# Sparse attention and spectral mix on one core: the first value rows through SyncE as fp32, rounded on chip

## The chip, the cores and the metric

The kernel runs on one core of one Trainium2 chip. The metric is the device time of one execution in microseconds (us). The number quoted for the kernel before is the median of three runs: 428.08 us, from 427.69 to 428.46 us.

## The reference, cut to what matters

Two stages follow one another. The first is a sparse attention over 8 batches, 8 heads, 576 positions and 64 columns. Heads 0 to 3 see the last 32 positions ("local"), heads 4 to 7 see every 32nd position ("strided"). The second stage treats the result as x (8 x 576 x 512): it takes a real Fourier transform along the sequence, multiplies the lowest 64 modes by complex 512 x 512 matrices, transforms back, adds, and applies one more matrix.

```python
mask_local = (rel >= 0) & (rel < stride)
mask_strided = (rel >= 0) & (pos[None, :] % stride == pos[:, None] % stride)
scores = np.where(masks[None, :, :, :], scores, -1000000000.0)
attn = softmax(scores); attn_out = np.matmul(attn, v)
...
X = np.fft.rfft(x, axis=1)
Yr = np.einsum('bmd,mde->bme', Xr, w_r) - np.einsum('bmd,mde->bme', Xi, w_i)
Yi = np.einsum('bmd,mde->bme', Xr, w_i) + np.einsum('bmd,mde->bme', Xi, w_r)
y = np.fft.irfft(Y, n=S, axis=1)
u = x + y
return u + np.maximum(u @ w_ch, 0.0)
```

Inputs and outputs are fp32. The two weight tensors w_r and w_i hold 64 x 512 x 512 numbers each, 134 MB together, and make up most of what is read.

## The kernel before, in words

All matmuls run in fp16 with fp32 sums. Every large input is therefore rounded on its way into SBUF, by a transfer that GpSimd issues (`nc.gpsimd.dma_start` from an fp32 tensor into an fp16 tile). These transfers form one list in program order on one queue, called q0 in the profile: first the strided rows of q, k and v, then, interleaved by hand, the weights (`w_fetch`, lines 182 to 190), the local rows (`load_loc`, line 229) and more strided rows. Eight semaphores are used in rotation, so a transfer of this list is issued only when the one eight places before it has landed. Some transfers also wait until TensorE has finished with the buffer that they overwrite.

The strided rows of one batch and one of q, k, v make a tile of 72 partitions by 2048 columns in `ring`: a partition holds 32 consecutive positions of one head. `load_str(b, nb)` loads partitions 0 to 63 with one transfer (line 220 for one batch, line 218 for two at once) and, for even b, partitions 64 to 71 of both batches of the pair with another (line 222, here called the tail, 64 KB in fp16). For b = 0 the list begins: v rows 0 to 63 (256 KB in fp16), v tail, q rows, q tail, k rows, k tail; then v, q and k rows of batch 1 without tails; then the pair of batches 2 and 3.

The constants lie in DRAM as fp16 and go through the two other queues: cI (identity for the transposes), cM6 and cM5 (masks of the strided scores) by ScalarE (q10 in the profile), cT (the Fourier table) and cMl (mask of the local scores) by SyncE (q1). After the rows of batch 1 GpSimd itself runs `strided_tokens` (lines 327 to 329), two memsets and a copy of cT, which has to have landed; the transfers that come later in its list stand behind that copy.

The computation of batch 0 begins with transposes of v (`str_v`, lines 276 to 283, in three column groups `JG` of 6, 5 and 5 blocks of 128 columns), which need rows and tail of v and cI. Ahead of them in program order VectorE clears `kzs[0]` (line 794). Later the strided stage runs over the 8 batches, then the local stage together with the first weights (`mode`, matmuls of line 597), then the second half of the weights, and at the end the last modes (line 630), the inverse transform and the output.

The weight tiles have five buffers of their own and three guests: the tile of mode pair 7 lies under the tag "YT" of the pool `big`, which later holds a spectrum.

Of the kernel before, what the change touches and what calls it, by code (L numbers as in the profile page):

```python
# [10 lines left out]
FP = mybir.dt.float32  # L11
# [12 lines left out]
JG = [(0, 6), (6, 11), (11, 16)]  # L24
# [32 lines left out]
def kernel(  # L57
# [10 lines left out]
    nc = tc.nc  # L68
# [3 lines left out]
    big = ctx.enter_context(tc.tile_pool(name="big", bufs=1))  # L72
# [5 lines left out]
    def psum_pools(**bufs):  # L78
        pctx.close()
        pss.clear()  # L80
        for n, c in bufs.items():
            pss[n] = pctx.enter_context(
                tc.tile_pool(name="ps_" + n, bufs=c, space=PSUM)
            )
# [22 lines left out]
    def const_load(eng, *which):  # L107
        for n in which:
            eng.dma_start(cs[n][:, 0 : hosts[names.index(n)].shape[1]], drams[n])
# [93 lines left out]
    def str_in(b, vi):  # L203
        return ring[0:72, 3 * (b % 4) + SLOT[vi], :]

    def loc_in(b, vi):
        t = ring[:, ds(2 * (b % 6), 2), :].rearrange("p n x -> p (n x)")
        return t[:, ds(1152 * vi, 1152)]

    def load_str(b, nb):  # L210
        for vi in (2, 0, 1):
            n = 3 * (b % 4) + SLOT[vi]
            two = ring[:, n : n + 4 : 3, :]
            src = SRC[vi][b - b % 2 : b - b % 2 + 2, 4:8].rearrange(
                "b h (c r) d -> (h c) b (r d)", r=32
            )
            if nb == 2:
                nc.gpsimd.dma_start(two[0:64], src[0:64])
            else:
                nc.gpsimd.dma_start(ring[0:64, n, :], src[0:64, b % 2])  # L220
            if b % 2 == 0:
                nc.gpsimd.dma_start(two[64:72], src[64:72])
# [27 lines left out]
    def act_copy(out, in_):  # L250
        nc.scalar.activation(out=out, in_=in_, func=ACTF.Copy)  # L251
# [511 lines left out]


    psum_pools(tp=3, sc=3, av=2)
    load_str(0, 1)
    const_load(nc.scalar, "cI", "cM6", "cM5")
    load_str(1, 1)
    const_load(nc.sync, "cT", "cMl")
    strided_tokens()  # L770
    load_str(2, 2)
    w_fetch()

    def str_front(b):
        return [
            lambda: str_v(b, 0), lambda: str_v(b, 1),
            lambda: str_v(b, 2), lambda: str_q(b, 0),
            lambda: str_back(b, 0),
            lambda: str_back(b, 1), lambda: str_q(b, 1),
            lambda: str_k(b, 0),  # L780
            lambda: str_k(b, 1), lambda: str_k(b, 2),
        ]

    def loc_front(b):
# [6 lines left out]
            lambda: loc_back(b, 0), lambda: loc_back(b, 1),  # L791
        ]

    nc.vector.memset(kzs[0], 0.0)
    first = str_front(0)
    for i, w in enumerate(first):
# [170 lines left out]
    for n, i in enumerate([3, 5, 7] + list(range(8, 21))):  # L967
        b, t = n // 2, n % 2 * 2
# [144 lines left out]
```

## Time and profile before

| what | value |
|---|---|
| median of 3 runs | 428.08 us (427.69 to 428.46) |
| span of the profiled execution, first to last instruction | 426.7 us |
| median less span | 1.4 us |
| PE busy | 346.4 us (81%) |
| DVE / ACT / POOL busy | 234.7 / 218.3 / 110.7 us |
| time that packets of q0 took, as a share of 16 DMA engines | 96.2% |
| read from HBM | 162.83 MB |

The profile gives the span of one execution; no separate total for that execution is given, so the 1.4 us between its span and the median of the runs is taken as what lies around it. PE is TensorE, DVE VectorE, ACT ScalarE, POOL GpSimd and SP SyncE. "Idle before, releaser" tells which instruction or transfer ended an engine's idle time. The bytes of the DMA rows are those written: a rounding transfer reads twice as many as it writes.

### The profile page before, as it was taken

To read this page: it belongs to the slowest core of one execution; us is meant where nothing else is said; L and a number is where in the kernel's file an instruction comes from. 1 tells how busy PE (TensorE), PEld (TensorE's weight loads), DVE (VectorE), ACT (ScalarE), POOL (GpSimd) and SP (SyncE) were. 2 spreads that over 40 slices of the span, in tenths; PEclk is the share of its full clock that TensorE was granted. 3 is DMA by queue.
4 is the path that set the end of the run, shared out by engine and by line. 5 is a ranking of instruction groups with operands and counts; after the bars stand their busy time and mean duration, and the time that the engine had idled before them with its cause. 6 is when DMAs were issued, how large, how long until landed. Compare 5 with 4: busy or idle time off the path is not lost.

```text
span 426.7 us, 9768 instructions
## 1 busy us (share of the span) xinstructions
PE 346.4 (81%) x4167; PEld 208.2 (49%) x4167; DVE 234.7 (55%) x466; ACT 218.3 (51%) x390; POOL 110.7 (26%) x196
## 2 busy tenths in 40 slices
PE   2977878769999698889768788878788867889993
PEld 2866767554656365566433344435444423445330
DVE  3788778851355154356113246746676354655884
ACT  1687678643656356556642235423442444443872
POOL 8332333322423222222222322222232222210000
PEclk9999899967999689999995889989999979989997
DMA  8999999999999999999999999999999999995698
GB/s 150 210 212 212 213 213 213 211 211 211 214 213 213 213 213 215 212 214 215 210 214 211 213 214 213 210 213 215 212 213 214 213 213 214 214 212 105 244 355 287
DMA packets 30938, 91.62 MB, mean 215 GB/s; under 512 B 4464, under 2 KB 5232, under 8 KB 30896
## 3 DMA queue, kind: packets, MB, share of 16 engines
q0 software_dynamic: 25168, 81.28, 96.2%
q1 hardware_dynamic: 4976, 9.13, 5.9%
q10 hardware_dynamic: 752, 0.61, 0.5%
q8 instruction: 32, 0.52, 0.5%
q14 instruction: 10, 0.08, 0.0%
HBM read 162.83 MB, written 9.44 MB: 404 GB/s over the span
## 4 chain that ended last, share of the span: by engine, by line
DMA 47%; PE 29%; DVE 14%; ACT 5%; issue 3%; DVEq 0%; POOL 0%; ACTq 0%; POOLq 0%
DMA wt<-in_moe_w_i_dram 38%; DMA wt<-in_moe_w_r_dram 7%; PE y L597 5%; DVE xb L241 3%; DVE kz L283 3%; PE p L987 2%; ACT X L251 2%; PE sc L532 2%; PE tp L413 2%; PE sc L459 1%; PE p L1001 1%; PE y L532 1%; PE p L760 1%; DVE yy L752 1%; DVE rec L240 1%
## 5 line engine op out<-in xcount | busy, mean ns | idle before, releaser
L597 PE MATMUL y<-wt,X 128*32 128x512 f16 (+1 forms) x448 | 70.9, 430 | 20.1 <-DMA wt<-in_moe_w_i_dram 20.1
L186 POOL DMA_DIRECT2D wt<-in_moe_w_r_dram x59 | 34.7, 588 | 126.4 <-PE y L597 56.3
L186 POOL DMA_DIRECT2D wt<-in_moe_w_i_dram x60 | 35.4, 590 | 68.3 <-DMA wt<-in_moe_w_i_dram 44.4
L597 PEld LDWEIGHTS <-X 128*32 128x32 f16 (+1 forms) x448 | 28.1, 140 | 39.4 <-DMA wt<-in_moe_w_i_dram 18.6
L727 DVE COPY xo<-tp 128x512 f16<-128x512 f16 x32 | 22.1, 691 | 36.8 <-PE tp L725 36.8
L726 ACT ACTIVATE v<-sc 128x512 f16<-128x512 f32 x32 | 19.1, 597 | 44.2 <-PE sc L717 44.2
L717 PE MATMUL sc<-w_cp,xT 128*128 128x512 f16 x128 | 36.9, 410 | 1.9 <-DVE xT L690 1.9
L489 ACT ACTIVATE PL<-sc 128x480 f16<-128x480 f32 (+1 forms) x48 | 27.0, 578 | 21.3 <-PE sc L475 21.0
L241 DVE TENSOR_TENSOR xb<-av,rec 90x256 f16<-90x256 f32 (+2 forms) x80 | 36.0, 450 | 2.8
L240 DVE RECIPROCAL rec<-av 90x4 f32<-90x4 f32 (+2 forms) x80 | 14.6, 183 | 39.3 <-PE av L504 28.2
L251 ACT ACTIVATE yr<-y 128x512 f16<-128x512 f32 x28 | 16.7, 597 | 36.8 <-PE y L597 35.6
L961 DVE TENSOR_TENSOR xo<-p,xo 128x1024 f16<-128x1024 f32 x16 | 19.6, 1225 | 21.7 <-PE p L760 21.7
L420 DVE COPY qT<-tp 128x576 f16<-128x576 f16 x16 | 11.9, 752 | 34.7 <-PE tp L413 34.7
L251 ACT ACTIVATE v<-p 128x1024 f16<-128x1024 f32 x16 | 16.4, 1023 | 23.1 <-PE p L760 23.1
L378 ACT ACTIVATE PL<-sc 90x360 f16<-90x360 f32 (+1 forms) x48 | 22.7, 490 | 7.0 <-PE sc L371 6.4
L251 ACT ACTIVATE v<-tp 128x640 f16<-128x640 f16 (+1 forms) x24 | 19.0, 807 | 11.8 <-PE tp L447 9.3
L413 PE MATMUL tp<-cI_s,ring 64*64 64x64 f16 x864 | 22.4, 197 | 2.7 <-DVE qT L420 2.4
L459 PE MATMUL sc<-cMl_s,cI_s 128*128 128x480 f16 (+1 forms) x48 | 19.4, 405 | 4.5 <-ACT PL L489 2.9
L276 PE MATMUL tp<-cI_s,ring 72*128 72x72 f16 x256 | 15.4, 207 | 8.7 <-DMA ring<-in_v_dram 7.1
L413 PEld LDWEIGHTS <-ring 64*64 64x64 f16 x864 | 17.5, 110 | 9.4 <-issue 5.4
L251 ACT ACTIVATE kz<-tp 64x360 f16<-64x360 f16 (+1 forms) x32 | 18.9, 592 | 6.2 <-PE tp L413 5.2
L1013 ACT ACTIVATE rl<-p 128x1024 f32<-128x1024 f32 (+1 forms) x19 | 18.4, 979 | 5.7 <-PE p L1001 3.1
(142 smaller groups left out, 737.9 us busy)
## 6 DMA issues: line engine op xcount, KB each, us to landing
wt<-in_moe_w_i_dram POOLq DMA_DIRECT2D x60, 512.0 KB, 18.8
wt<-in_moe_w_r_dram POOLq DMA_DIRECT2D x59, 512.0 KB, 17.7
out_dram<-osb SPq DMA_DIRECT2D x15, 512.0 KB, 3.4
ring<-in_v_dram POOLq DMA_DIRECT2D x8, 288.0 KB, 13.4
ring<-in_q_dram POOLq DMA_DIRECT2D x8, 288.0 KB, 13.6
ring<-in_k_dram POOLq DMA_DIRECT2D x8, 288.0 KB, 13.1
ring<-in_v_dram POOLq DMA_DIRECT2D x3, 512.0 KB, 14.8
ring<-in_q_dram POOLq DMA_DIRECT2D x3, 512.0 KB, 14.8
```

The source lines that it names most:

```text
L186: nc.gpsimd.dma_start(dst, rows)
L241: nc.vector.tensor_tensor(out=dst, in0=val.rearrange("p h (q c) -> p h c q", c=4), in1=rec[0:n, 0:pieces] .to_broadcast((n, pieces, 64)) . ...
L251: nc.scalar.activation(out=out, in_=in_, func=ACTF.Copy)
L378: nc.scalar.activation(out=PS[0:n, ds(POFF[t], 4 * n)], in_=scp[0:n, 0 : 4 * n], func=ACTF.Exp, scale=SCALE,)
L413: nc.tensor.transpose(tp[ds(64 * hp, 64), ds(64 * i, 64)], qn[ds(64 * hp, 64), ds(64 * (9 * g + i), 64)], idn[ds(64 * hp, 64), ds(64 * hp, ...
L459: nc.tensor.matmul(scp[:, 0 : n * times].rearrange("p (h x) -> p h x", h=times), idn, mask_rows("cMl", n, times), start=True, stop=False,)
L489: nc.scalar.activation(out=dst, in_=src, func=ACTF.Exp, scale=SCALE)
L597: nc.tensor.matmul(yp[ds(a, 32), :], Xh[half][pr, c].rearrange("p b r (h m) -> p (b r h) m", h=2)[:, :, mm % 32], wt[pr, XC[c], :], start= ...
L717: nc.tensor.matmul(vp, xT[:, ch], w_chs["cp"][:, ch, :], start=(ch == 0), stop=(ch == 3),)
L726: nc.scalar.activation(out=v0, in_=vp, func=ACTF.Copy)
L727: nc.vector.tensor_copy(out=xo.rearrange("p (h q c) -> p h q c", h=2, c=4), in_=tp[:, 0:512].rearrange("p (h c q) -> p h q c", h=2, c=4),)
L961: nc.vector.tensor_tensor(out=xo, in0=up[:, 0:n], in1=xo, op=AluOp.add)
```

## The change

The v rows 0 to 63 of batch 0 leave GpSimd's list. SyncE loads them as fp32, without rounding, into a new tile `first32` (128 x 2048 fp32, of which 64 partitions are used) as the first transfer of its queue, ahead of cT and cMl. Three copies then round them into their place in `ring`, one for each column group: groups 0 and 2 on VectorE, group 1 on ScalarE. The copies stand ahead of the clearing of `kzs[0]` in program order. GpSimd's list now begins with the v tail, followed by the q rows. `first32` uses the tag "YT", so that the weight tile of mode pair 7 comes after it in the same memory.

```diff
+    first32 = big.tile([128, 2048], FP, tag="YT", name="first32")
+
+    def first_rows():
+        src = v[0, 4:8].rearrange("h (c r) d -> (h c) (r d)", r=32)
+        nc.sync.dma_start(first32[0:64], src[0:64])
+
+    def first_round(j):
+        cols = ds(128 * JG[j][0], 128 * (JG[j][1] - JG[j][0]))
+        dst, src = str_in(0, 2)[0:64, cols], first32[0:64, cols]
+        if j == 1:
+            act_copy(dst, src)
+        else:
+            nc.vector.tensor_copy(out=dst, in_=src)
+
     def load_str(b, nb):
...
             if nb == 2:
                 nc.gpsimd.dma_start(two[0:64], src[0:64])
-            else:
+            elif b or vi != 2:
                 nc.gpsimd.dma_start(ring[0:64, n, :], src[0:64, b % 2])
...
     psum_pools(tp=3, sc=3, av=2)
+    first_rows()
     load_str(0, 1)
     const_load(nc.scalar, "cI", "cM6", "cM5")
...
+    for j in range(3):
+        first_round(j)
     nc.vector.memset(kzs[0], 0.0)
```

## The prediction

> **What bounds the kernel now.** I read the page first: its DMA rows and its chain.
>
> ```profile
> DMA  8999999999999999999999999999999999995698
> q0 software_dynamic: 25168, 81.28, 96.2%
> DMA 47%; PE 29%; DVE 14%; ACT 5%; issue 3%; DVEq 0%; POOL 0%; ACTq 0%; POOLq 0%
> ```
>
> The DMA engines are busy from the second slice to the 36th, nearly all of it in GpSimd's queue q0, and DMA is the largest share of the chain. A busy share can still hide holes, so next comes the table by stretches (columns: stretch and its length, then PE, PEld, DVE, ACT and POOL busy time with counts, the granted clock, the DMA share, GB/s written).
>
> ```profile
> 1.50:2.00 0.50, 0.00 (x0) 0.00 (x0) 0.50 (x1) 0.00 (x0) 0.50 (x2) 1.00 0.46 58
> 2.00:2.50 0.50, 0.00 (x0) 0.00 (x0) 0.14 (x1) 0.39 (x1) 0.50 (x2) 1.00 0.83 255
> 2.50:3.00 0.50, 0.00 (x0) 0.00 (x0) 0.00 (x0) 0.50 (x1) 0.50 (x2) 1.00 1.54 267
> 3.00:3.50 0.50, 0.00 (x0) 0.00 (x0) 0.00 (x0) 0.40 (x1) 0.50 (x2) 1.00 1.07 66
> 3.50:4.00 0.50, 0.00 (x0) 0.00 (x0) 0.00 (x0) 0.00 (x0) 0.50 (x2) 1.00 0.24 33
> 4.00:4.50 0.50, 0.00 (x0) 0.00 (x0) 0.00 (x0) 0.00 (x0) 0.50 (x2) 1.00 0.95 164
> ...
> 110.00:160.00 50.00, 44.80 (x698) 28.36 (x696) 21.86 (x44) 28.23 (x55) 14.49 (x25) 0.90 1.07 213
> 210.00:260.00 50.00, 38.51 (x293) 19.45 (x294) 16.92 (x40) 16.67 (x32) 13.87 (x23) 0.83 1.07 213
> 310.00:360.00 50.00, 39.28 (x292) 19.46 (x291) 26.60 (x46) 21.30 (x34) 12.99 (x22) 0.93 1.06 213
> ```
>
> From 10 to 376 us every stretch writes 212 to 214 GB/s at a share of 1.06 to 1.09: one saturated stream, whatever the other engines do. The only holes are at the start, where 3.0 to 4.0 us carries 66 and 33 GB/s. So the last weight arrives at: start of the stream, plus its work, plus holes. To see whether the end follows the stream, I asked for TensorE's waits and its timeline near the end.
>
> ```profile
> PE y L597 <- DMA wt<-in_moe_w_i_dram: 20.1, 15, 3.5
> 377.24 0.64 PE L630 MATMUL y<-X,wt 128*128 128x16 f16 x16 [1.24 <-DMA wt<-in_moe_w_i_dram]
> ```
>
> TensorE waits 15 times for weights in line 597, 3.5 us at the longest, and at 377.24 us it has stood 1.24 us for the last weight but a few. From there to the end the chain is TensorE, VectorE and output. A shift of the stream by up to 1.24 us therefore shifts the end one for one; a shift of the attention by less than 3.5 us is swallowed by those waits. The chain's long "DMA" pieces, 14 to 20 us each, run from issue to landing and are mostly queueing: a weight transfer of 512 KB moves in 2.46 us (0.524 MB at 213 GB/s).
>
> Does a buffer release hold the stream back? I subtracted the end of each issue of q0 from the landing of the transfer before it. After the first 12 us the smallest difference is 5.9 us (issue at 107.46 us), and an issue needs 1.6 us to its first packet (1.23 to 2.81 us for the first). Releases have over 4 us to spare, so a stream that runs 1 us earlier is not stopped by them.
>
> **The change, part by part.** The stream's ledger is all that counts; the sum is made against the span of 426.7 us, and 1.4 us lie around it.
>
> *v rows out of q0.* 64 packets, 0.262 MB written; at 213 GB/s 1.23 us less work in the stream: -1.23.
>
> *Unused time at the start.* By the packet records the first packet of any queue starts at 1.67 us, and the first sixteen of q0 start between 2.81 and 3.92 us but all end between 4.07 and 4.47, where later ones take 0.32 us. Up to 4.07 us the engines had 2.40 us. Work in it: cT 128 packets of 51 ns, cMl 128 of 27, cI 128 of 18, cM6 128 of 16, over 16 engines 0.90 us, and sixteen q0 packets 0.32 us. Unused: 1.18 us. SyncE issues at 0.74 us, so its rows can lie there from 1.67 us. The first constant packets took up to 0.43 us instead of 0.05, so some 0.2 is lost in any case: -1.0. The other end: if the 1.2 us stall of the first q0 packets comes from touching v for the first time, the fp32 rows meet it themselves, and only 0.2 is filled.
>
> *fp32 rows.* 0.524 MB into 64 partitions, unrounded; no row shows such a transfer. The nearest by kind is cT, also unrounded but over 128 partitions: 1152 B in 51 ns on 16 engines, 361 GB/s, 1.45 us. A transfer at the stream's reading rate (426 GB/s) would take 1.23. The nearest by destination are rows 0 to 63 and weights of q0, which never write faster than 213 GB/s: 2.46 us. The tails decide which: 64 KB into eight partitions, and of the packets started between 5.2 and 5.4 us five took 0.79 to 1.27 us where 0.32 is usual. Few partitions do slow the writing here, so I take +2.46 and keep 1.23 as the other end.
>
> The Trainium skill speaks against the change at this place: "SBUF — State Buffer", section "Door 1: The DMA port swizzle", says that 64 partitions reach only 8 of 16 ports, some 218 GB/s at best, because a row's port does not depend on whether it lies in the lower or upper 32. By that page the rows are estimated at 2.41 us, and a model that looks at bytes read alone would say 1.23; the tails agree with the page.
>
> *In the shadow of the rows.* A transfer held to half rate by its destination leaves the engines about half free. Other queues can use that: the v tail (sixteen packets, 0.32 us, other partitions) and cI with cM6 (0.27 us) together 0.59; I take -0.5, with 0.3 as the low end. cT and cMl stand behind the rows in SyncE's own queue and cannot.
>
> *Sum:* -1.23 + 2.46 - 1.0 - 0.5 = -0.27 us. Best: -1.23 + 1.23 - 1.18 = -1.2. Worst: -1.23 + 2.46 - 0.2 - 0.3 = +0.7.
>
> **What is covered.** *GpSimd's queue* loses one issue (0.66 us) and, being one place shorter, no longer waits 0.84 us before the k rows of batch 1; the pairs of the eight-semaphore rotation are otherwise the same.
>
> ```profile
> 6.55 0.51 POOL L220 DMA_DIRECT2D ring<-in_k_dram  x1 [0.84 <-DMA ring<-in_v_dram]
> 7.05 0.17 POOL L327 MEMSET cT_s<- 128x64 f16 x1
> 7.14 0.14 POOL L328 MEMSET PL<- 128x18 f16 x1
> 7.19 1.16 POOL L329 COPY PL<-cT_s 128x576 f16<-128x576 f16 x1
> 8.29 0.59 POOL L218 DMA_DIRECT2D ring<-in_v_dram  x1
> ```
>
> It comes to the copy of cT at about 6 us. *SyncE's queue:* cT and cMl are issued 0.4 us later and flow behind four 8 KB packets on each engine. What happens to constants beside the running stream is seen on cM5, issued at 1.63 us:
>
> ```profile
> cM_s<-cM ACTq DMA_DIRECT2D x1, 22.5 KB, 5.5
> ```
>
> 5.5 us to land instead of 2.5, its eight packets on each engine taking turns with q0's of 0.32 us. With the rows done at about 4.3 us, cT's eight take 8 x 0.37 = 3.0 us and, with 0.5 from the last packet to the landing (cMl's), land near 7.8. GpSimd then waits about 1.8 us at line 329, with the pair of batches 2 and 3 behind it. That is covered: their first issue was at 8.29 us, and its bytes were due only when the k rows ended, about 13.5 us; less 1.6 us, the issue may start at 11.9, and cT may land at 10.7. *VectorE* rounds 768 and 640 columns: from 685 ns for 512 columns of fp32 (line 752) 1.03 + 0.86 us; *ScalarE* 640 columns from 597 ns for 512, 0.75 us. Behind VectorE's two stands the clearing of kz (1.07 us). With the rows landed at 4.8 us it is done at 7.8, against the first copy of transposed v at 7.67 before: at most about 0.8 us late if the rows land at 5.5, and hidden by the weight waits above. If that cover were gone it would cost those 0.8 us. *Tag YT:* the weight tile of modes 14 and 15 waits for copies that ended tens of us before.
>
> A second rule concerns the two VectorE copies: "SBUF — State Buffer", section "SBUF: two separate sides", warns that an fp32 copy within SBUF on VectorE keeps GpSimd from writing its descriptors. No such copy is in this trace; in sentences that the sum does not use, its price would be a GpSimd list that stands up to 1.9 us, beside a spare of 3.8 us at the tightest early issue.
>
> **Forecast and rivals.** About 0.2% (0.86 us) is what a measurement of this kernel can tell from no change.
>
> *Forecast (0.40):* -0.3 us, 427.8 us, inside that bound.
>
> *All unused time filled (0.28):* the rows run at the reading rate, or the stream's other queues fill their gaps wholly. Gain 0.9 to 1.2 us, time 426.9. For: the empty 3.0 to 4.0 us, and transfers of SyncE that start 1.1 us ahead of GpSimd's. Against: the slow tails.
>
> *The stall moves along (0.20):* the change doesn't bring the stream forward, because the first touch of v stalls the new queue. From 0.1 to 0.7 us more, 428.5. For: q0's first packets end together however late they start; against: packets of a first touch of q and k show no such common end. I leave 0.08 of it beyond +0.86 us.
>
> *The queue runs dry behind cT (0.12), slower:* place: the wait at line 329. It decides if cT lands after 10.7 us; every us beyond is a us of empty stream. If the engines gave SyncE's queue a turn only after every third q0 packet, cT would land at 4.3 + 8 x 1.02 + 0.5 = 13.0 us, 2.3 us too late: 427.8 + 2.3 = 430.1. Against: cM5 got its turns one for one.
>
> Faster 0.28; within the bound 0.40 + 0.12 = 0.52; slower 0.08 + 0.12 = 0.20. The range leaves out the dry queue and the far end of the stall: sums from -1.2 to +0.7, times 426.9 to 428.8, and 0.1 us of scatter at each end. The forecast's own range is 427.3 to 428.3.
>
> **What would show it.** Right: SyncE's 64 packets of 8 KB take about 0.6 us each and end near 4.3 us; q0 starts with the tail; no stretch after 5 us falls under 200 GB/s; the last weight lands 0.3 us earlier than now (391.94 us) and TensorE still waits near 377 us. Packets of 0.32 us would speak for the second case; first packets of over 1 us from 1.67 us for the third; a hole between 11 and 14 us, and a copy of line 329 that starts after 10.7 us, for the fourth. The forecast is wrong in kind if the last landing moves by more than 1.2 us, or if the end does not move with it.

## The result and the profile after

The changed kernel takes 429.01 us (median of 18 runs) against 427.96 us for the kernel before: 1.05 us slower by the medians, ratio 1.003 with a 95% interval of 1.0021 to 1.0038, which is 0.9 to 1.6 us. The forecast of 427.8 us had the wrong sign, and its range ended at 428.9.

One profile of each is too little to see this. Where a run lists both its time and its span, they lie about 1.8 us apart, so the first profile of the kernel before (span 426.7 us) was an execution of about 428.5 us, slower than its median, and the profile of the changed kernel (span 426.8, 428.55 us) one of its faster ones. Second profiles gave 426.0 and 427.0 us. So the total is left to the runs. In the profiles I read the landing of the q rows of batch 1, a transfer of GpSimd's list near the start, which repeats to about 0.1 us (single packets before it do not).

The table by stretches of the changed kernel, with the columns of the one before:

```profile
1.50:2.00 0.50, 0.00 (x0) 0.00 (x0) 0.00 (x0) 0.00 (x0) 0.50 (x1) 1.00 0.21 47
2.00:2.50 0.50, 0.00 (x0) 0.00 (x0) 0.00 (x0) 0.41 (x1) 0.50 (x2) 1.00 0.99 215
2.50:3.00 0.50, 0.00 (x0) 0.00 (x0) 0.00 (x0) 0.50 (x1) 0.50 (x2) 1.00 0.56 229
3.00:3.50 0.50, 0.00 (x0) 0.00 (x0) 0.00 (x0) 0.38 (x1) 0.50 (x2) 1.00 1.41 360
3.50:4.00 0.50, 0.00 (x0) 0.00 (x0) 0.00 (x0) 0.00 (x0) 0.50 (x2) 1.00 0.89 185
4.00:4.50 0.50, 0.00 (x0) 0.00 (x0) 0.00 (x0) 0.00 (x0) 0.50 (x2) 1.00 0.64 121
4.50:5.00 0.50, 0.00 (x0) 0.00 (x0) 0.00 (x0) 0.00 (x0) 0.50 (x2) 1.00 1.11 198
```

The hole of 66 and 33 GB/s between 3 and 4 us is gone, as the change intends. But what fills it is the rows themselves, and behind them the constants. By the packet records the 64 row packets of 8 KB start between 2.10 and 4.26 us and end at 4.76 (4.59 in a second profile); most packets of the constants of SyncE and ScalarE run behind them, until 6.7 us; and GpSimd's queue, whose first packets started at 2.81 us before, starts its first data packet at 5.38 us (4.95 in the second profile). What that means on the engines is in the timeline:

```profile
0.74 0.58 SPq L214 DMA_DIRECT2D first<-in_v_dram  x1
5.75 0.64 POOL L341 MEMSET cT_s<- 128x64 f16 x1
5.83 0.58 POOL L342 MEMSET PL<- 128x18 f16 x1
5.76 1.00 DVE L222 CAST ring<-first 64x768 f16<-64x768 f32 x2 [5.76 <-DMA first<-in_v_dram]
6.74 1.14 POOL L343 COPY PL<-cT_s 128x576 f16<-128x576 f16 x1 [0.32 <-DMA cT_s<-cT]
7.72 1.12 PE L290 MATMUL tp<-cI_s,ring 72*128 72x72 f16 x16 [7.72 <-DMA ring<-in_v_dram]
7.88 0.59 POOL L232 DMA_DIRECT2D ring<-in_v_dram  x1
```

The first transposes of the kernel before, for comparison:

```profile
7.12 1.11 PE L276 MATMUL tp<-cI_s,ring 72*128 72x72 f16 x16 [7.12 <-DMA ring<-in_v_dram]
```

The rows land only at 5.74 us, where the prediction had 4.8. The copies follow at once, but TensorE waits until 7.72 us for the v tail, the first transfer of GpSimd's list, which was issued at 1.34 us and landed at 7.59; before, the transposes started at 7.12. GpSimd waits 0.32 us for cT and issues the pair of batches 2 and 3 at 7.88 us in place of 8.29. Nothing is short of issued work: GpSimd is early, its queue is late. The q rows of batch 1, transfer number eight of the list before and seven now, land at 13.66 and 13.77 us in the two profiles, against 12.89 and 12.86 before: 0.84 us later, though 1.23 us of work had been taken out ahead of them.

The end follows: the last weight lands at 392.29 and 392.50 us, against 391.94 and 391.46 in the two profiles of before, and TensorE still waits for weights:

```profile
PE y L611 <- DMA wt<-in_moe_w_i_dram: 22.6, 17, 3.5
PE y L644 <- DMA wt<-in_moe_w_i_dram: 4.9, 4, 2.5
```

Line 611 is line 597 of before, 644 is 630.

### The profile page after: what moved, and what is told of

Same layout as the page of the kernel before. It is cut to its first block, busy times and chain, and to the rows that moved or that the text cites. A ratio compares the mean times of both kernels' runs of the same rounds, so it can differ in the third digit from the quotient of the medians.

```text
span 426.8 us, 9774 instructions
## 1 busy us (share of the span) xinstructions
PE 340.9 (80%) x4167; PEld 205.2 (48%) x4167; DVE 235.9 (55%) x468; ACT 218.8 (51%) x391; POOL 111.1 (26%) x195
## 4 chain that ended last, share of the span: by engine, by line
DMA 55%; PE 15%; DVE 4%; issue 2%; ACT 2%; DVEq 0%; POOL 0%; ACTq 0%; POOLq 0%
DMA wt<-in_moe_w_i_dram 41%; DMA wt<-in_moe_w_r_dram 10%; DMA ring<-in_v_dram 4%; PE y L611 3%; PE p L1004 2%; PE p L1018 1%; DVE yy L766 1%; PE sc L731 1%; PE p L1009 1%; ACT X L265 1%; PE u L1009 1%; PE y L546 1%; PE p L774 1%; PE sc L473 1%; DVE xb L255 1%
## 5 line engine op out<-in xcount | busy, mean ns | idle before, releaser
L611 PE MATMUL y<-wt,X 128*32 128x512 f16 (+1 forms) x448 | 68.7, 417 | 22.6 <-DMA wt<-in_moe_w_i_dram 22.6
```

Of the source, the lines that this page charges most:

```text
L611: nc.tensor.matmul(yp[ds(a, 32), :], Xh[half][pr, c].rearrange("p b r (h m) -> p (b r h) m", h=2)[:, :, mm % 32], wt[pr, XC[c], :], start= ...
```

## The experiments

Each is compared with runs of the kernel before on the same chip. Three theories were on trial: that the end follows the stream of GpSimd's queue and the rows cost their time there (stream); that the later start of the attention is what costs (attention); and, within the first, what makes the rows dear: their destination of 64 partitions, or a slow start that meets every first transfer.

**The rows left out.** Edit of the kernel before:

```diff
-            else:
+            elif b or vi != 2:
                 nc.gpsimd.dma_start(ring[0:64, n, :], src[0:64, b % 2])
...
+    nc.vector.memset(str_in(0, 2)[0:64], 0.0)
     nc.vector.memset(kzs[0], 0.0)
```

> The v rows 0 to 63 of batch 0 are loaded by no queue; VectorE writes zeros in their place, so this part of the input is missing from the computation. Stream theory (the end follows the weight stream, and the rows cost the change its time at the stream's start): 0.262 MB at 213 GB/s is gone, so about 1.2 us faster than before, 426.8 us, and some 2.2 us faster than the changed kernel. Attention theory (the changed kernel is slower because the first transposes start 0.6 us later): the transposes start earlier here, so a gain too, but of 0.6 us or less.

Measured: 426.93 against 427.86 us, ratio 0.9973 (0.9961 to 0.9985), so 0.6 to 1.7 us faster. In its profile the q rows of batch 1 land at 11.70 us, 1.19 earlier than in the kernel before, and the last weight at 390.75, 1.19 earlier than in the first profile of before and 0.71 earlier than in the second. The step from stream to end is as predicted, and so is the term of -1.23 us for the rows taken out of GpSimd's list. The rows put back as fp32 then cost 1.96 and 2.07 us by the landings of the q rows (13.66 and 13.77 less 11.70), 2.1 us by the medians, and by the ratios 1.0030 - 0.9973 = 0.0057 or 2.4 us.

**A later attention.** The kernel before with one in-place copy:

```diff
+    act_copy(str_in(0, 2)[:, 0:512], str_in(0, 2)[:, 0:512])
     nc.vector.memset(kzs[0], 0.0)
```

> The kernel before with one more step: ScalarE copies the first 512 columns of batch 0's v onto themselves before the first transposes, which delays the start of the attention by about 0.65 us and leaves all transfers as they were. Attention theory: slower by 0.6 to 1.0 us, 428.6 to 429.0 us. Stream theory: no change, 428.0 us within 0.3.

Measured: 427.97 against 427.86 us, ratio 1.0005 (0.9996 to 1.0015). The delay came out longer than meant, since the table load of ScalarE now stands ahead of the copy:

```profile
8.81 1.14 PE L276 MATMUL tp<-cI_s,ring 72*128 72x72 f16 x16 [8.81 <-ACT ring L251]
```

That is 1.69 us behind the kernel before, where the changed kernel is 0.60 behind. The attention theory falls: more than the delay of the changed kernel is swallowed.

**The copies left out**, with all transfers as in the changed kernel:

```diff
-    for j in range(3):
-        first_round(j)
+    nc.vector.memset(str_in(0, 2)[0:64], 0.0)
     nc.vector.memset(kzs[0], 0.0)
```

> The changed kernel with all its transfers, but the three rounding copies left out; VectorE writes zeros to their place at the start, so the v rows of this batch are missing from the computation. Stream theory (the transfer of the rows is the whole cost): 429.0 us within 0.4, as the changed kernel. If the copies cost time (they hold up GpSimd's memsets, 0.64 us where 0.17 is usual, and the later clearing of kz): back towards 428.2 us.

Measured: 429.31 us, ratio 1.0031 (1.0021 to 1.0041). The copies cost nothing that can be measured; the cost lies with the transfers.

**Constants first**, then the rows:

```diff
-    first_rows()
     load_str(0, 1)
...
     const_load(nc.sync, "cT", "cMl")
+    first_rows()
```

> The changed kernel with cT and cMl ahead of the fp32 rows on SyncE's queue. Stream theory: the engines have the same bytes to move before GpSimd's queue comes up, so 428.6 to 429.2 us, as the changed kernel; the rows land about 0.7 us later, at 6.4 us. If the displaced constants (GpSimd waiting for cT) were the cause: back to 428 us.

Measured: 428.63 us, ratio 1.0024 (1.0011 to 1.0037). cT lands at 3.1 us here, as in the kernel before, and most of the loss stays: a late cT is not the cause. The rows now run from 3.2 to 7.1 us beside the start of GpSimd's queue and land at 8.38 us, not at the expected 6.4; the q rows of batch 1 land at 13.67 us, where the changed kernel has them. In this order the gap is in its old place:

```profile
3.00:3.50 0.50, 0.00 (x0) 0.00 (x0) 0.00 (x0) 0.40 (x1) 0.50 (x2) 1.00 0.52 56
3.50:4.00 0.50, 0.00 (x0) 0.00 (x0) 0.00 (x0) 0.00 (x0) 0.50 (x2) 1.00 0.42 51
```

Rows issued at 1.61 us did not fill it: two of their packets start at 3.21 and 3.23 us, the next one at 3.90.

**All partitions.** The same 512 KB as one transfer over 128 partitions:

```diff
-        nc.sync.dma_start(first32[0:64], src[0:64])
+        nc.sync.dma_start(
+            first32[:, 0:1024], src[0:64].rearrange("p (x c) -> (p x) c", x=2)
+        )
```

> The changed kernel with the same 512 KB of fp32 v rows loaded by one transfer over all 128 partitions (each row's halves on two neighbouring partitions); the copies have the same sizes, but columns end up in the wrong places, so the v of this one batch is scrambled. Destination theory (64 partitions hold the rows to half rate, 2.4 us): the rows end about 1.2 us earlier, near 3.5 us; GpSimd's first packets start near 4 us in place of 5.2; time 427.6 to 428.0, about 1.2 us under the changed kernel. Start theory (the rows cost their time because every new transfer starts slowly, wherever it writes): 429.0 us, as the changed kernel.

Measured: 428.41 us against 427.79, ratio 1.0018 (1.0006 to 1.0029). The stretches of its profile:

```profile
1.50:2.00 0.50, 0.00 (x0) 0.00 (x0) 0.00 (x0) 0.00 (x0) 0.50 (x1) 1.00 0.30 37
2.00:2.50 0.50, 0.00 (x0) 0.00 (x0) 0.00 (x0) 0.39 (x1) 0.50 (x2) 1.00 0.00 1
2.50:3.00 0.50, 0.00 (x0) 0.00 (x0) 0.00 (x0) 0.50 (x1) 0.50 (x2) 1.00 0.63 229
3.00:3.50 0.50, 0.00 (x0) 0.00 (x0) 0.00 (x0) 0.39 (x1) 0.50 (x2) 1.00 1.06 421
3.50:4.00 0.50, 0.00 (x0) 0.00 (x0) 0.00 (x0) 0.00 (x0) 0.50 (x2) 1.00 0.98 389
```

Two things are to be read here. The first is the time of the packets themselves. Over all partitions a packet of 4 KB takes 0.159 us from 2.5 us on, and the stretches from 3 to 4 us write 421 and 389 GB/s. In the changed kernel the packets of 8 KB that start between 2.7 and 3.1 us take 0.31 to 0.41 us, about the same per byte, but most of those that start after 3.3 us take 0.60 to 0.66, twice as long. Summed and spread over 16 engines, the rows' packets took 2.03 us in the changed kernel (2.10 in its second profile) and 1.37 us here. So the destination does set the rate of the later packets. The size of the packets is not what helps: in the run with two queues below, packets of 4 KB into partitions 64 to 127 take 0.25 to 0.32 us from 3.5 us on, but for one.

The second is that this saving of 0.7 us is all there is, not 1.2. The time is 0.6 us under the changed kernel by the medians (the two intervals overlap), the q rows of batch 1 land at 13.24 us, 0.4 to 0.5 earlier, and GpSimd's first data packet starts at 4.39 us. From first start to last end the rows take 2.59 us, hardly less than the 2.66 and 2.50 us of the changed kernel, because there is a pause at their start: three row packets start at 1.83 to 1.86 us and take 0.65 to 0.67, and until 2.4 us nothing else starts (1 GB/s), not even ScalarE's cI, whose own packets had begun before. Against the kernel without rows, the rows cost 1.5 us here (1.9 by the ratios), at least the 1.37 us of their packets. Neither theory met its number.

**Two halves.** Columns 0 to 1023 to partitions 0 to 63, the others to 64 to 127, as two transfers. In the first kernel SyncE issues both; in the second, whose edit is shown, each of two queues issues one. The copies gather the halves.

```diff
-        nc.sync.dma_start(first32[0:64], src[0:64])
+        for x in range(2):
+            (nc.scalar if x else nc.sync).dma_start(
+                first32[ds(64 * x, 64), 0:1024], src[0:64, ds(1024 * x, 1024)]
+            )
```

> The changed kernel with the fp32 rows split into columns 0 to 1023 on partitions 0 to 63 and columns 1024 to 2047 on partitions 64 to 127, two transfers of SyncE; the copies bring both halves to partitions 0 to 63. If the destination of 64 partitions sets the 2.4 us of the rows: packets of 4 KB at about 0.16 us, the rows end 0.8 to 1.2 us earlier, GpSimd's first packets start near 4.2 us in place of 5.2, and the time is 0.6 to 1.2 us under the changed kernel, 427.8 to 428.4. If the destination does not matter: no change, 429.0 us.

Measured: 429.21 us, ratio 1.0035 (1.0019 to 1.005). The rows' packets run from 2.10 to 6.17 us. Up to 3.0 us they take 0.16 to 0.29 us, but for one; then GpSimd's queue starts, at 2.99 us, and its first eight packets, to 3.5 us, take 0.81 to 1.75 us. From there the two queues run side by side, and the q rows of batch 1 land at 14.52 us.

> The changed kernel with columns 0 to 1023 loaded to partitions 0 to 63 by SyncE and columns 1024 to 2047 to partitions 64 to 127 by ScalarE, each ahead of its constants, so that both halves of SBUF are written at once. Destination theory: the rows end near 3.5 us as with all partitions, 427.6 to 428.2 us, at or a little under the kernel before. Start theory: 429 us. The constants cI and cM6 come later by 0.6 us, which neither theory counts.

Measured: 429.40 us, ratio 1.0033 (1.0021 to 1.0046). Both expectations of the destination theory fail, though the destination matters. For the second run the packet records tell why: even from two queues the halves run mostly one after the other, the first from 2.1 to 3.6 us, the second from 3.0 to 4.7, together 0.524 MB in 2.6 us or 200 GB/s. Only one transfer that spans all partitions was faster. By the medians these two are 0.2 to 0.4 us slower than the changed kernel, by the ratios no different from it; cT landed at 9.2 us in the first of them, at 6.7 in the second, and the second moved ScalarE's constants behind the start of GpSimd's queue.

**The gap itself.** The kernel before with 8 KB of v, 512 bytes from each of 16 rows, read by SyncE ahead of everything:

```diff
+    def touch_rows(which):
+        warm = big.tile([128, 2048], FP, tag="YT", name="warm")
+        for vi in which:
+            t = warm[0:16, ds(128 * vi, 128)]
+            src = SRC[vi][0, 4:8].rearrange("h (c r) d -> (h c) (r d)", r=32)
+            nc.sync.dma_start(t, src[0:16, 0:128])
...
     psum_pools(tp=3, sc=3, av=2)
+    touch_rows((2,))
     load_str(0, 1)
```

> The kernel before, with one more transfer of SyncE ahead of its constants: 512 bytes from each of 16 rows of v, 8 KB in all, into memory that nothing reads. First-touch theory (the 1.2 us of the first GpSimd packets is the first access to v, which the fp32 rows of the changed kernel meet themselves, so that the gap moves along with them): GpSimd's first packets take 0.32 us from 2.8 us on and all landings come 0.6 to 1.0 us earlier, 427.0 to 427.4 us. Queue theory (the stall belongs to the start of GpSimd's queue, whatever it reads): first packets of 1.2 us as before, 427.9 us.

Measured: 428.06 against 427.89 us, ratio 1.0009 (1.0 to 1.0018): no gain. Its stretches:

```profile
2.00:2.50 0.50, 0.00 (x0) 0.00 (x0) 0.14 (x1) 0.37 (x1) 0.50 (x2) 1.00 0.38 66
2.50:3.00 0.50, 0.00 (x0) 0.00 (x0) 0.00 (x0) 0.50 (x1) 0.50 (x2) 1.00 1.41 294
3.00:3.50 0.50, 0.00 (x0) 0.00 (x0) 0.00 (x0) 0.41 (x1) 0.50 (x2) 1.00 1.08 161
3.50:4.00 0.50, 0.00 (x0) 0.00 (x0) 0.00 (x0) 0.00 (x0) 0.50 (x2) 1.00 0.93 180
```

The gap of 66 and 33 GB/s at 3 to 4 us has gone: 41 data packets of GpSimd's queue start by 4.0 us instead of 16 (19 in the second profile of before), and four of its first sixteen take over 0.9 us instead of ten (thirteen). So the slow start of that queue depends on what was read before it. The low stretch at 2.0 to 2.5 us, 66 GB/s where the kernel before moves 255, is not that gap in a new place. The small read of v shows no stall of its own: its 16 packets take 25 to 29 ns each. What is missing there is cT, which stands behind it in SyncE's queue and is issued 0.47 us later than before:

```profile
0.74 0.41 SPq L215 DMA_DIRECT2D warm<-in_v_dram  x1
1.21 0.41 SPq L109 DMA_DIRECT2D cT_s<-cT  x1
```

The constants of SyncE come later by that much, and their last packets run after 4.5 us, beside GpSimd's queue. The q rows of batch 1 land at 12.89 us, exactly as before. The same with q and k touched behind v:

> As the run with v touched, with 8 KB of q and of k touched in the same way behind it. First-touch theory: 426.8 to 427.4 us, at least as early as with v alone. Queue theory: 427.9 to 428.1 us.

Measured: 428.33 us, ratio 1.0009 (0.9999 to 1.0018). No gain either, and the q rows of batch 1 land only at 13.59 us, although none of the first sixteen packets of GpSimd's queue takes over 0.6 us; cT is issued at 2.14 us here and lands at 6.99. Of the two theories for these runs the second had the time right, and the first had right that GpSimd's queue need not start slowly. That the gap travels with the first access to v is not shown, though. In the run with two halves from SyncE, v was being read from 2.10 us on without a pause, and GpSimd's first packets stalled all the same; here the small reads of v did not stall at all. What makes the pause stays open. What all these runs show is that none of them got time out of it.

**Second profiles** of both kernels, for the repeat values used above:

> The kernel before once more, for a second profile: first GpSimd packet near 2.8 us, the last weight landing within 0.6 us of 391.9.

Measured: first GpSimd packet at 2.8 us, q rows of batch 1 landed at 12.86, last weight at 391.46 us (391.94 in the first profile), span 426.0 us.

> The changed kernel once more, for a second profile. Stream theory: the q rows of batch 1 land 0.8 us later than in the kernel before, and so does the last weight, within the 0.4 us that profiles of one kernel differ by. If the loss were elsewhere: the last weight lands with the kernel before, and the time is lost after it.

Measured: q rows of batch 1 at 13.77 us, last weight at 392.50, span 427.0 us. In twelve of the thirteen profiles of this study the span is the landing of the last weight plus 34.4 to 34.6 us (34.7 in the first profile of before). Nothing is lost after the stream.

None of these versions beats the kernel before, apart from the one that leaves the rows out.

## Why the prediction was wrong

*Right: the bound.* The end follows the last weight (34.4 to 34.7 us behind it in every profile), the last weight follows the start of the stream as far as profiles can tell (rows left out: 1.19 us at the start, 1.19 or 0.71 at the last weight), GpSimd's queue stays fed, and a later attention costs nothing.

*Right: the rows out of q0, -1.23 us.* Measured -0.9 by the medians, -1.2 by the ratio, -1.19 in the landings.

*Nearly right: the price of the fp32 rows, +2.46 us.* Their packets took 2.03 and 2.10 us on 16 engines in the two profiles, and 2.66 and 2.50 us from first start to last end; over all partitions the packets took 1.37. The row that decided it, the slow tails into eight partitions, was the right one to trust. The rule weighed there, of the Trainium skill's "SBUF — State Buffer", section "Door 1: The DMA port swizzle", holds for the later packets: 0.60 to 0.66 us for 8 KB into 64 partitions is 199 to 218 GB/s on 16 engines, against 412 GB/s at 0.159 us for 4 KB into 128. The packets before them, 0.31 to 0.41 us, were not held to it. Its neighbour section "Can I just issue two DMAs to hit both halves?" says that two such transfers follow one another; the run with two queues agrees for the most part: 2.1 to 3.6 and then 3.0 to 4.7 us.

*Wrong: "Unused time at the start", -1.0 us.* This is the step that failed. I counted 1.18 us in which the engines had no work and took 1.0 of it as free for SyncE's rows. (The first packet starts at 1.73 us, not at 1.67, so the count should have been 1.12.) It was not free. The rows cost the stream 1.96 and 2.07 us by the landings, which is all that their packets took; by the prediction's own price of 2.46 the two credits, 1.5 us in the sum, were worth 0.4 to 0.5 together. With the constants first the rows stood ready and the gap stayed; with v touched ahead, GpSimd's queue started faster and its q rows landed no earlier. In the changed kernel GpSimd's first packets are no longer slow (0.32 us, but for one of the first sixteen), but the time went elsewhere. The rows' first packet starts at 2.10 us, 0.4 later than cT's did, of which 0.22 is SyncE's longer issue (0.58 us instead of 0.36); their first twelve packets take 0.49 to 0.79 us; and the packets of cT, behind them, mostly 0.07 to 0.1 us instead of 0.05. The prediction had this outcome as the "other end" of the term, 0.2 us filled, and as a rival, "the stall moves along", at 0.20. Its reason, a stall that belongs to the first touch of v, is neither confirmed nor excluded by these runs.

*Wrong: "In the shadow of the rows", -0.5 us.* That a transfer at half rate leaves the engines half free for other queues was assumed, and no run here shows it. No data packet of GpSimd's queue started until the rows had ended (5.38 us behind 4.76, 4.95 behind 4.59 in the second profile), although the v tail had been issued at 1.34. cI ran ahead of the rows, as it would have anyway. Only cM6 (3.65 to 4.88 us, 0.13 us of work) and the first packets of cT, from 4.40 us, ran beside them. Even its low end, 0.3, was too large.

With both terms at nothing the ledger is -1.23 + 2.46 = +1.23 us, and +0.8 to +0.9 with the 2.03 and 2.10 us that the packets took; measured were 1.05 (0.9 to 1.6) in the runs and 0.84 in the landings. How the missing 1.5 us divides between the two terms was not measured. The worst case of the text, +0.7, kept 0.2 and 0.3 of them, and so the range closed below the result. The rival that came nearest had only 0.08 beyond the bound of 0.86 us.

*The slower rival, the queue that runs dry behind cT,* did not happen: cT landed at 6.69 us, well before 10.7, and the wait at GpSimd's copy was 0.32 us (6.93 and 0.95 in the second profile). What was wrong in it is smaller: cT's packets did not alternate with q0's for 3 us, because q0 had not begun.

*The copies* were cheaper than estimated: 0.55 and 0.53 us on VectorE against 1.03 and 0.86, 0.74 on ScalarE against 0.75. The second rule, of the Trainium skill's "SBUF — State Buffer", section "SBUF: two separate sides", is about descriptors, and no issue of GpSimd fell beside the copies but the last 0.07 us of one, so these runs do not show it. What did stand beside them were GpSimd's memsets: those of 0.17 and 0.14 us took 0.64 and 0.58 (0.24 and 0.20 with the copies left out, and in the second profile, where the copies came behind them). It cost no time, since the list had room.

## What to carry to other kernels

When a stream of transfers sets the end, a hole at its start should be credited only if it is known what makes it; here the first transfers were ordered in several ways, the hole changed its place and form, and none of them got time out of it. Moving a load to another queue also means losing what the first queue did on the way: here the rounding transfer wrote half the bytes, and unrounded rows into 64 partitions took about twice the time that they saved. Before crediting "time beside" a slow transfer, look for a row in which another queue's packets really run beside one.

## What the runs showed of the hardware that was not expected

- At the start there is a pause of some 0.5 to 1 us in which hardly a packet of any queue starts, but not in every order of the first transfers: at 3 to 4 us in the kernel before (66 and 33 GB/s) and with the constants first (56 and 51), at 2.0 to 2.5 us with the rows over all partitions (1 GB/s), but of only 0.1 us (2.10 to 2.21) with 8 KB of v read first. GpSimd's first sixteen packets took up to 1.26 us in the kernel before and at most 0.6 us when v, q and k had been touched. What makes it was not found.
- A queue with issued work can stand still behind another: GpSimd's first data packet came at 5.38 us behind SyncE's rows and most of the constants, though its transfer was issued at 1.34 us, earlier than cT (1.37 us), whose packets ran from 4.40. With the constants first, and with the rows in two halves, rows and GpSimd's packets did mix (from 3.2 to 7.1 and from 3.0 to 6.2 us). What decides between the two is not shown.
- Rows of 8 KB into 64 partitions take 0.31 to 0.41 us each between 2.7 and 3.1 us and mostly 0.60 to 0.66 after 3.3 us; the same bytes over 128 partitions hold 0.159 us per 4 KB from 2.5 us on.
